# Attention and mixture-of-experts on one core: the first loads cut by the step that reads them, one buffer cleared by GpSimd, fewer unread products

## The chip, the core and the metric

The kernel runs on one core of a Trainium2 chip. The core has TensorE (PE, and PEld for its weight loads), VectorE (DVE), ScalarE (ACT), GpSimd (POOL) and SyncE (SP, which here issues most DMAs), and 16 DMA engines. The metric is the device time of one execution in microseconds (us): the median of several runs.

## The reference

Windowed attention feeds a routed mixture of experts. The attention part, cut to what matters:

```python
scores = scale * np.matmul(q, k.transpose(0, 1, 3, 2))      # q, k, v: 8 x 8 heads x 576 x 64
rel = pos[:, None] - pos[None, :]
mask_plain = (rel >= 0) & (rel < 32)                        # heads 0 to 3
mask_dil = (rel >= 0) & (rel < 128) & (rel % 4 == 0)        # heads 4 to 7
scores = np.where(masks[None, :, :, :], scores, -1000000000.0)
attn = np.exp(scores - np.max(scores, axis=-1, keepdims=True))
attn = attn / (np.sum(attn, axis=-1, keepdims=True) + 1e-09)
x = np.matmul(attn, v)                                      # then 4608 tokens of 512 numbers
# each token goes to one of 4 groups and one of its 4 experts, by the largest logit;
# out = g_w * e_w * (relu(x @ w1[g, e]) @ w2[g, e])
```

## The kernel before

The attention part is a loop over 36 steps, s = 0 to 35, written out by hand. Three steps share a load group g = s // 3, and a step takes the part jl = s % 3 of it. `qb[g % 3]` holds the group's queries, `kb[g % 2]` its keys, `vt[g % 3]` its values. The third buffers of q and v lie in the two weight buffers `wa`, so the trace calls `vt[2]` "wa". Step 0 reads its keys from a small buffer of its own, `k0t`, which also lies in "wa".

Pass s of the loop issues, on TensorE: a product that writes the masks into the score buffer (L254), the scores of step s (L273), the product of step s - 2's probabilities with the values (`av`, L315), the transposes of step s - 1's probabilities (L303), and those of step s - 3's result (L393). VectorE takes the maximum of the scores and subtracts it (L283, L285), ScalarE takes the exponential (L296) and copies the transposed probabilities out (L304). So the scores of step 3 stand ahead of `av` of step 1, in the same pass.

`keep_busy(n)` issues n products of the masks (L239) into a buffer that nothing reads, after the mask product of steps 0 and 1.

`av` reads the values twice: as loaded (`vt`) and shifted by half a block (`vs`). GpSimd makes `vs` with `shift_v`: the even half (partitions 64 to 127) takes the same part j of the group, the odd half takes part j - 1, or the last part of the group before. For group 0 it is called as `shift_v(0, 0, 1)` and `shift_v(0, 1, 3)`, so one GpSimd instruction makes the even half of parts 1 and 2 together (64x2x1040, which the trace calls 64x2080).

`carry_k(g)` fills the first 256 columns of `kb`. For every third group, GpSimd clears them (L119, 128x2x256, 128x512 in the trace); otherwise ScalarE copies them from the other buffer (L121). The clearing for group 3 writes `kb[1]`, whose first columns step 3 of group 1 reads.

TensorE, VectorE, ScalarE and SyncE follow the order of the program text here or a hand order; on GpSimd a scheduler of the language places the instructions, and each engine works through its own list in that order. SP issues the loads in the order in which they are written. `masks` comes in two DMAs: parts 0 and 1 by ACT, parts 2 to 5 by POOL; step 2 is the first that reads part 2.

```python
load_q(0, 1, 3)
load_k(0)
load_v(0, (0, 1, 3))
nc.gpsimd.dma_start(masks[:, 2:], cm[:, 2:])
load_k(1)
load_q(1)
load_q(2)
load_v(1)
```

After the steps come the routing of the last tokens, the choice of experts, and 18 pieces of expert work, with matmuls all the way.

Of the kernel before, what the change touches and what calls it, by code (L numbers as in the profile page):

```python
# [17 lines left out]
P = 128  # L18
# [38 lines left out]
def moe_attention_kernel(ctx, tc, q, k, k0, v, cmask, wgate, wpack, out):  # L57
    nc = tc.nc
# [34 lines left out]
    NQ, NK, NPT = 3, 2, 2  # L93
# [6 lines left out]
    vt = [qp.tile([P, 2, 3, 8, 65], F32, name=f"vt{i}") for i in range(2)]  # L100
    vt.append(wa32[1][:, 0:VW].rearrange("p (w j s c) -> p w j s c", w=2, j=3, s=8))
    vs = [qp.tile([P, 2, 3, 8, 65], F32, name=f"vs{i}") for i in range(2)]
    kb = [qp.tile([P, 2, KW], F32, name=f"kb{i}") for i in range(NK)]
# [6 lines left out]
    def load_q(g, j0=0, j1=3):  # L110
        nc.sync.dma_start(qb[three(g)][:, j0:j1], q[g, :, j0:j1])

    def load_k(g, halves=(0, 1)):
        for w in halves:
            nc.sync.dma_start(kb[g % NK][w:P:2, w, 256:], k[g, w])

    def carry_k(g):
        if g % 3 == 0:
            nc.gpsimd.memset(kb[g % NK][:, :, 0:256], 0.0)  # L119
        else:  # L120
            nc.scalar.copy(kb[g % NK][:, :, 0:256], kb[(g - 1) % NK][:, :, 3 * 256 : 4 * 256])  # L121

    def load_v(g, cuts=(0, 3)):
        for j0, j1 in zip(cuts, cuts[1:]):
            for r in range(2):
                nc.sync.dma_start(vt[three(g)][r:P:2, r, j0:j1], v[g, 64 * r : 64 * r + 64, j0:j1])
# [20 lines left out]
    for i, t in enumerate(kb):  # L147
        nc.vector.memset(t[:, 0], 0.0)
        nc.scalar.activation(t[:, 1], id32[:, 0:1].broadcast_to([P, KW]), AF.Copy, scale=0.0)
        if i == 0:  # L150
            nc.vector.memset(vt[0][:, 0], 0.0)
            nc.gpsimd.memset(vt[0][:, 1], 0.0)
    flat = lambda t: t.rearrange("p w j s c -> p (w j s c)")
    nc.scalar.activation(flat(vt[1]), id32[:, 0:1].broadcast_to([P, VW]), AF.Copy, scale=0.0)
    for w in range(2):
        nc.sync.dma_start(k0t[w:P:2, w, 0 : 8 * 96], k0[w])
    load_q(0, 1, 3)
    load_k(0)
    load_v(0, (0, 1, 3))
    nc.gpsimd.dma_start(masks[:, 2:], cm[:, 2:])  # L160
    load_k(1)
    load_q(1)
    load_q(2)
    load_v(1)

# [68 lines left out]
    def keep_busy(n):  # L234

        t = psA.tile([P, 2, 512], F32, name="idle", tag="o")
        m = masks[:, 0:2].unsqueeze(1).broadcast_to([P, 2, 2, 128])
        for i in range(n):
            nc.tensor.matmul(t[:, i % 2].rearrange("p (u m c) -> p u m c", u=2, m=2), idb, m, start=True, stop=True)  # L239

    def slot():
        credit[0] = min(credit[0] + rate[0], 2 * rate[0])
        while routes and not gate and credit[0] > 0:
            took = run(routes)
            if took in (2, 3):
                gate.append(took)
            elif took not in (None, 1):
                credit[0] -= took

    def scores(n):  # L250
        g, jl, J = n // 3, n % 3, n % NJ
        s = psS.tile([P, 4, 2, 64], F32, name="s", tag="s")
        m = masks[:, MASK_OF.get(J, 1), :]
        nc.tensor.matmul(  # L254
            s.rearrange("p (t u) w k -> p t (u w) k", t=2),
            idb,
            m.rearrange("p (t k) -> p t k", t=2).unsqueeze(2).broadcast_to([P, 2, 4, 64]),
            start=True,
            stop=False,
        )  # L260
        if n < 2:
            keep_busy((3, 10)[n])
        qv = qb[three(g)][:, jl]
        if n == 0:
            kv, ev0 = k0t[:, :, 0 : 8 * 96].rearrange("p w (s b k) -> p w b s k", s=8, k=32), 2
        else:
            kv, ev0 = kb[g % NK].rearrange("p w (b s k) -> p w b s k", s=8, k=32), 4
        for c in range(4):
            for bb in range(2):
                for a in range(2):  # L270
                    sl, j = bb * 4 + c, bb * 2 + a
                    first, step = jl + a, ev0 - a
                    nc.tensor.matmul(  # L273
                        s[32 * j : 32 * j + 32, c].rearrange("p w k -> p (w k)"),
                        qv[:, (sl * 2 + a) * 32 : (sl * 2 + a) * 32 + 32],
                        kv[:, :, first : first + step + 1 : step, sl],
                        start=False,
                        stop=(c == 3),
                    )
        s = s.rearrange("p c w k -> p (c w) k")  # L280
        d = ap.tile([P, 4, 64, 2], F32, name="d", bufs=2)
        mx = ap.tile([P, 8], F32, name="mx")
        nc.vector.tensor_reduce(mx, s, axis=AX.X, op=ALU.max)  # L283
        slot()
        nc.vector.tensor_tensor(  # L285
            d.rearrange("p c k w -> p c w k"),
            s.rearrange("p (c w) k -> p c w k", w=2),
            mx.rearrange("p (c w) -> p c w", w=2).unsqueeze(3).broadcast_to([P, 4, 2, 64]),
            ALU.subtract,
        )  # L290
        slot()
        dd[n] = d

    def softexp(n):
        p = dd.pop(n)
        nc.scalar.activation(p, p, AF.Exp, scale=SCALE)  # L296
        st[n] = p

    def transpose_p(n):
        p = st.pop(n)  # L300
        t = psT[0].tile([P, 4, P], F32, name="t", tag="t")
        for c in range(4):
            nc.tensor.transpose(t[:, c, :], p[:, c].rearrange("p k w -> p (k w)"), id32)  # L303
        nc.scalar.copy(pt[n % NPT], t)  # L304

    def av(n):
        g, jl = n // 3, n % 3
        o = psA.tile([P, 2, 512], F32, name="o", tag="o")
        for c in range(4):
            for bb in range(2):  # L310
                for a in range(2):
                    j = bb * 2 + a
                    t = vt[three(g)] if a else vs[g % 2]
                    at = 130 * (c % 2)
                    nc.tensor.matmul(  # L315
                        o[32 * j : 32 * j + 32, c // 2, at : at + 130],
                        pt[n % NPT][:, c, 32 * j : 32 * j + 32],
                        t[:, :, jl, bb * 4 + c, :],
                        start=True,
                        stop=True,  # L320
                    )
        oo[n] = o
# [589 lines left out]
    def expert(r):  # L912
        ev[r] = nc.sync.value_load(ordi[0:1, r : r + 1], min_val=0, max_val=NE - 1)
# [36 lines left out]
    for s in range(NT + 3):  # L950
        ripe = bool(gate)
        if s < NT:
            scores(s)
        if s % 3 == 2 and s // 3 + 2 < NT // 3:
            load_k(s // 3 + 2, (0,))
        if s % 3 == 0 and 2 <= s // 3 + 1 < NT // 3:
            load_k(s // 3 + 1, (1,))
        if s % 3 == 1 and 1 <= s // 3 + 1 < NT // 3:
            carry_k(s // 3 + 1)
        if s % 3 == 0 and NQ <= s // 3 + 2 < NG:  # L960
            load_q(s // 3 + 2) if s // 3 + 2 < NG - 1 else None
        if s // 3 + 2 == NG - 1:
            load_q(NG - 1, s % 3, s % 3 + 1)
        if 0 <= s - 2 < NT:
            av(s - 2)
            if ripe:
                gate.clear()
        if start:
            n = start[0]
            routes.append(route(n, turned_logits(n)))  # L970
            rate[0] = RATE[n]
        if 0 <= s - 1 < NT:
            transpose_p(s - 1)
        if s < NT:
            softexp(s)
        if s == 0:
            nc.vector.memset(flat(vt[2]), 0.0)
        if 0 <= s - 3 < NT:
            transpose_x(s - 3)
        if s % 3 == 1 and 2 <= s // 3 + 2 < NG - 1:  # L980
            load_v(s // 3 + 2)
        if s // 3 + 1 == NG - 1 and s % 3 < 2:
            load_v(NG - 1, ((0, 2), (2, 3))[s % 3])
        if 0 <= s - 2 < NT:
            normalise(s - 2)
        if start:
            n = start.pop()
        if gate == [3]:
            gate.clear()
        slot()  # L990
        if s % 3 == 0 and s // 3 + 1 < NT // 3:
            shift_v(s // 3 + 1, 0, 2)
        if s % 3 == 1 and s // 3 + 1 < NT // 3:
            shift_v(s // 3 + 1, 2, 3)
        for r in picked:
            if r not in ev:
                expert(r)
        if s == min(WSTEPS):
            wq.append(prefetch())
        if s == NT - 1:  # L1000
            eb.append(early(0, new_x(fe, EARLY[0]), fe, EARLY[0]))
        run(eb, EARLY_STEPS.get(s, 0))
        run(wq, WSTEPS.get(s, 1))
        if s >= 3 and (s - 3) % NJ == NJ - 1:
            bp = (s - 3) // NJ
            if bp < NBP - 1:
                start.append(bp)
        run(eq)
# [242 lines left out]
```

## Time and profile before

| | |
|---|---|
| median of 3 runs | 556.91 us (556.44 to 557.72) |
| profiled execution | 565.16 us, its span 563.4 us |
| TensorE busy | 537.1 us, 95% of the span |
| VectorE, ScalarE, GpSimd busy | 66%, 56%, 43% |
| attention steps | first product at 4.17 us, the masks of step 35 at 136.27 us |
| memory | 106.16 MB read, 19.29 MB written |

The span is what the profiler saw of the program; the execution's own time holds 1.8 us more. A busy share counts an instruction from its start to its modelled end. In a row of the timeline, "[1.00 <-DMA qb<-q]" says that the engine stood idle for 1.00 us before the row and that a landing of q into qb ended it. The queue of an engine that issues DMAs is written with a q: SPq, POOLq, ACTq.

### The profile page before, as it was taken

Reading aid. Unit: us, or ns where it says so; the run is one execution under the profiler, and the core shown is the slowest. Engines: PE = TensorE matmul, PEld = TensorE weight load, DVE = VectorE, ACT = ScalarE, POOL = GpSimd, SP = SyncE. Lnnn points to the kernel's source line nnn. Section 1 sums busy time; section 2 is a strip of 40 time slices with the busy share of each in tenths; the row PEclk is TensorE's granted clock in tenths of the full one; section 3 lists DMA queues with packets and bytes.
Section 4 is the critical chain, followed back from the end, with each engine's and each line's share of the span. In section 5 each row is a group of like instructions: output and inputs, shape, how many; then the busy total and the mean of one; then the engine's idle time right before and its main releaser. Section 6 shows DMA issues by size and latency. Waiting matters only on the chain. (4 is left out here: it accounts for less than half of the span.)

```text
span 563.4 us, 16475 instructions
## 1 busy us (share of the span) xinstructions
PE 537.1 (95%) x6577; PEld 384.8 (68%) x6577; DVE 369.9 (66%) x842; ACT 316.3 (56%) x563; POOL 241.1 (43%) x219
## 2 busy tenths in 40 slices
PE   6899999998898999999999999999999999999995
PEld 4777878786765765657666667575656756787883
DVE  8776786877787226574859597755647477658640
ACT  6555556567663335564646565564646567647741
POOL 6796566758958232603041513224160531221212
PEclk9999999999999999999999999999999999999999
DMA  8988988798592716978787786979697699898841
GB/s 284 407 288 278 320 268 279 233 317 290 162 305 55 259 41 127 335 180 258 185 286 165 271 211 226 255 225 293 175 315 199 217 295 276 293 333 229 257 113 30
DMA packets 79265, 134.31 MB, mean 238 GB/s; under 512 B 42988, under 2 KB 52630, under 8 KB 79186
## 3 DMA queue, kind: packets, MB, share of 16 engines
q1 hardware_dynamic: 72258, 113.65, 66.5%
q0 software_dynamic: 6784, 19.51, 10.4%
q8 instruction: 53, 0.87, 0.6%
q14 instruction: 26, 0.21, 0.1%
q10 hardware_dynamic: 144, 0.07, 0.0%
HBM read 106.16 MB, written 19.29 MB: 223 GB/s over the span
## 5 line engine op out<-in xcount | busy, mean ns | idle before, releaser
L818 POOL DMA_INDIRECT out<-yr,sent x31 | 38.4, 1238 | 220.0 <-ACT yr L817 202.0
L762 DVE SCALAR_TENSOR_TENSOR hl<-a,hh 128x256 f16<-128x256 f32 (+13 forms) x144 | 60.7, 424 | 97.6 <-ACT hh L761 77.4
L754 PE MATMUL a<-xs,wb1h 128*128 128x256 f16 (+7 forms) x576 | 97.9, 275 | 2.6 <-DVE hl L762 2.5
L754 PE MATMUL a<-xs,wa 128*128 128x304 f16 (+7 forms) x864 | 97.5, 272 | 1.5 <-issue 0.8
L761 ACT ACTIVATE hh<-a 128x256 f16<-128x256 f32 (+13 forms) x144 | 55.4, 388 | 72.1 <-PE a L754 55.3
L754 PEld LDWEIGHTS <-wa 128*128 128x128 f16 x864 | 79.0, 98 | 19.0 <-issue 2.5
L847 PEld LDWEIGHTS <-hh 128*128 128x128 f16 x480 | 46.9, 98 | 54.7 <-issue 1.2
L663 DVE SCALAR_TENSOR_TENSOR wa<-w,wa 128x1024 f16<-128x1024 f32 x57 | 69.1, 1230 | 18.5 <-ACT wa L667 14.6
L754 PE MATMUL a<-xs,wb1l 128*128 128x256 f16 (+7 forms) x288 | 78.3, 275 | 0.0
L847 PE MATMUL y<-wa,hh 128*128 128x512 f16 x240 | 73.9, 379 | 0.5 <-issue 0.5
L667 ACT ACTIVATE wa<-w 128x1024 f16<-128x1024 f32 x64 | 66.9, 1055 | 11.3 <-DMA w<-wpack 8.8
L754 PEld LDWEIGHTS <-wb1h 128*128 128x128 f16 x576 | 55.0, 98 | 15.6 <-issue 3.4
L817 ACT ACTIVATE yr<-y,cs 128x512 f32<-128x512 f32 (+3 forms) x31 | 21.3, 687 | 56.1 <-issue 26.4
L693 POOL DMA_INDIRECT xr<-xd,sent x41 | 42.1, 1026 | 19.2 <-issue 11.0
L847 PE MATMUL y<-wb2h,hh 128*128 128x512 f16 x120 | 45.6, 380 | 0.0
L847 PE MATMUL y<-wb2h,hl 128*128 128x512 f16 x120 | 45.5, 379 | 0.0
L847 PE MATMUL y<-wb2l,hh 128*128 128x512 f16 x120 | 45.5, 379 | 0.0
L847 PE MATMUL y<-wa,hl 128*128 128x512 f16 x120 | 45.5, 379 | 0.0
L663 DVE SCALAR_TENSOR_TENSOR wb2l<-w,wb2h 128x1024 f16<-128x1024 f32 x29 | 36.3, 1281 | 13.7 <-ACT wb2h L667 13.7
L304 ACT COPY pt<-t 128x512 f32<-128x512 f32 x36 | 21.0, 584 | 37.8 <-PE t L303 37.7
L315 PE MATMUL o<-vs,pt 128*32 128x130 f32 x576 | 39.9, 273 | 2.3 <-DVE own L498 0.9
L283 DVE TENSOR_REDUCE mx<-s 128x8 f32<-128x512 f32 x36 | 24.7, 687 | 24.5 <-PE s L273 24.4
(207 smaller groups left out, 1088.2 us busy)
## 6 DMA issues: line engine op xcount, KB each, us to landing
w<-wpack SPq DMA_DIRECT2D x128, 512.0 KB
kb<-k SPq DMA_DIRECT2D x24, 384.0 KB
vt<-v SPq DMA_DIRECT2D x14, 390.0 KB
qb<-q SPq DMA_DIRECT2D x7, 768.0 KB
xd<-x SPq DMA_DIRECT2D x24, 192.0 KB
wa<-v SPq DMA_DIRECT2D x6, 390.0 KB
wa<-q SPq DMA_DIRECT2D x3, 768.0 KB
xd<-x SPq DMA_DIRECT2D x32, 48.0 KB
```

The lines of the kernel that those rows point to most:

```text
L283: nc.vector.tensor_reduce(mx, s, axis=AX.X, op=ALU.max)
L304: nc.scalar.copy(pt[n % NPT], t)
L315: nc.tensor.matmul(o[32 * j : 32 * j + 32, c // 2, at : at + 130], pt[n % NPT][:, c, 32 * j : 32 * j + 32], t[:, :, jl, bb * 4 + c, :], st ...
L663: nc.vector.scalar_tensor_tensor(l, w32, SW, h, ALU.mult, ALU.subtract)
L667: nc.scalar.mul(parts(i)[0], w32s[i], SW)
L693: nc.gpsimd.indirect_dma_start(out=xr[0:n], out_offset=None, in_=xd[0:known, :], in_offset=bass.IndirectOffsetOnAxis(ap=ent[0:n, t : t + 1 ...
L754: nc.tensor.matmul(a[:, 0:cap], ww[:, c * FF + f * P : c * FF + f * P + P], xx[:, c, 0:cap], start=(i == 0), stop=(i == len(mm) - 1),)
L761: nc.scalar.activation(hh[:, f, 0:cap], a[:, 0:cap], AF.Relu)
L762: nc.vector.scalar_tensor_tensor(hl[:, f, 0:cap], a[:, 0:cap], 0.0, hh[:, f, 0:cap], ALU.max, ALU.subtract)
L817: nc.scalar.activation(yr[0:n, :], yp[0:n, :], AF.Copy, scale=cs[0:n, t : t + 1])
L818: ins = nc.gpsimd.indirect_dma_start(out=out, out_offset=bass.IndirectOffsetOnAxis(ap=ent[0:n, t : t + 1], axis=0), in_=yr[0:n, :], in_off ...
L847: nc.tensor.matmul(yp, h[:, f, t * P : t * P + n], ww[:, f * DM : f * DM + DM], start=(i == 0), stop=(i == len(mm) - 1),)
```

## The change

Three things change. The loads of group 0 and group 1 are cut by the part that a step reads, and go out in the order of the steps (`load_k_part` is new); one column block of `kb[0]` that no step reads is not loaded any more. The clearing of `vt[2]` moves from VectorE, behind step 0, to GpSimd, ahead of the DMA of masks 2 to 5. `keep_busy` of step 1 issues 1 product instead of 10; that of step 0 keeps its 3.

```diff
+    def load_k_part(g, j0, j1, h0=0, h1=2):
+
+        part = lambda a: a.rearrange("p (h c) -> p h c", h=2)[:, h0:h1, 256 * j0 : 256 * j1]
+        for w in range(2):
+            nc.sync.dma_start(part(kb[g % NK][w:P:2, w, 256:]), part(k[g, w]))
+
...
             nc.gpsimd.memset(vt[0][:, 1], 0.0)
+            nc.gpsimd.memset(vt[2].rearrange("p w j s c -> p (w j s c)"), 0.0)
...
-    load_q(0, 1, 3)
-    load_k(0)
-    load_v(0, (0, 1, 3))
+    load_q(0, 1, 2)
+    load_k_part(0, 1, 2)
+    load_k_part(0, 0, 1, 0, 1)
+    load_v(0, (0, 1))
+    load_q(0, 2, 3)
+    load_k_part(0, 2, 3)
+    load_v(0, (1, 2))
     nc.gpsimd.dma_start(masks[:, 2:], cm[:, 2:])
-    load_k(1)
-    load_q(1)
+    load_k_part(1, 0, 1)
+    load_q(1, 0, 1)
+    load_v(0, (2, 3))
+    load_k_part(1, 1, 3)
+    load_q(1, 1, 3)
     load_q(2)
     load_v(1)
...
-            keep_busy((3, 10)[n])
+            keep_busy((3, 1)[n])
...
-        if s == 0:
-            nc.vector.memset(flat(vt[2]), 0.0)
```

The order of the instructions shows three places. On SP, at the start of the program before the change, each row is one DMA, or two where it ends in x2:

```order
L111 DMA qb0_108<-q 128x512
L156 DMA wa0_91<-k0 64x768 x2
L111 DMA qb0_108<-q 128x1024
L115 DMA kb0_114<-k 64x1536 x2
L126 DMA vt0_110<-v 64x520 x2
L126 DMA vt0_110<-v 64x1040 x2
L115 DMA kb1_115<-k 64x1536 x2
L111 DMA qb1_109<-q 128x1536
L111 DMA wa0_91<-q 128x1536
L126 DMA vt1_111<-v 64x1560 x2
```

And on SP with the change, down to the same values of group 1:

```order
L111 DMA qb0_108<-q 128x512
L163 DMA wa0_91<-k0 64x768 x2
L111 DMA qb0_108<-q 128x512
L121 DMA kb0_114<-k 64x2x256 x2
L121 DMA kb0_114<-k 64x256 x2
L132 DMA vt0_110<-v 64x520 x2
L111 DMA qb0_108<-q 128x512
L121 DMA kb0_114<-k 64x2x256 x2
L132 DMA vt0_110<-v 64x520 x2
L121 DMA kb1_115<-k 64x2x256 x2
L111 DMA qb1_109<-q 128x512
L132 DMA vt0_110<-v 64x520 x2
```

The queries of group 1 that step 3 reads were part of the 13th DMA on SP and are now the 18th; the DMAs ahead of them are smaller.

On GpSimd, the opening of the program with the change; `wa1` is where `vt[2]` lies:

```order
L152 MEMSET wa0_91 128x768
L158 MEMSET vt0_110 128x1560
L159 MEMSET wa1_92 128x3120
L171 DMA masks_89<-cmask 128x512
L183 AFFINE_SELECT upper_161<-ones_159 128x128
```

Before, the row of `wa1` was not there, and the DMA of the masks followed the clearing of `vt0` at once.

On GpSimd a little later, the shifts of group 0's values and what follows them, before the change:

```order
L136 MEMSET vs0_112 64x2x520
L131 TENSOR_SCALAR vs0_112<-vt0_110 64x2x520
L134 TENSOR_SCALAR vs0_112<-vt0_110 64x2x520
L131 TENSOR_SCALAR vs0_112<-vt0_110 64x2x1040
L134 TENSOR_SCALAR vs0_112<-vt0_110 64x2x520
L138 TENSOR_SCALAR vs1_113<-vt0_110 64x2x520
L119 MEMSET kb1_115 128x2x256
```

And with the change (L137 is the even half, L140 the odd one, L125 the clearing by `carry_k`):

```order
L142 MEMSET vs0_112 64x2x520
L137 TENSOR_SCALAR vs0_112<-vt0_110 64x2x520
L140 TENSOR_SCALAR vs0_112<-vt0_110 64x2x520 x2
L125 MEMSET kb1_115 128x2x256
L137 TENSOR_SCALAR vs0_112<-vt0_110 64x2x1040
L144 TENSOR_SCALAR vs1_113<-vt0_110 64x2x520
```

The clearing of `kb1`'s first columns for group 3 stood behind all shifts of group 0; it now stands ahead of the one that makes the even half of parts 1 and 2. On VectorE, ScalarE and TensorE nothing else moves, but that a copy of 128x64 (`low`) now follows the first maximum on VectorE instead of standing ahead of it.

## Rows read from the trace of the kernel before

**Rows 1.** The page's busy times: engine, us, share of the span, instructions.

```profile
PE 537.1 (95%) x6577; PEld 384.8 (68%) x6577; DVE 369.9 (66%) x842; ACT 316.3 (56%) x563; POOL 241.1 (43%) x219
```

**Rows 2.** Timeline of PE, 0 to 20 us: start, us, operation, idle before.

```profile
4.17 0.59 PE L254 MATMUL s<-masks,idb 128*128 128x512 bf16 x1 [4.17 <-DMA masks<-cmask]
...
8.01 0.61 PE L254 MATMUL s<-masks,idb 128*128 128x512 bf16 x1
8.41 2.58 PE L239 MATMUL idle<-masks,idb 128*128 128x512 bf16 x10
10.92 1.08 PE L273 MATMUL s<-kb,qb 128*32 128x128 f32 x32
11.94 0.66 PE L303 MATMUL t<-id,d 128*128 128x128 f32 x4
12.43 0.38 PE L254 MATMUL s<-masks,idb 128*128 128x512 bf16 x1
12.74 1.08 PE L273 MATMUL s<-kb,qb 128*32 128x128 f32 x32
13.63 0.27 PE L315 MATMUL o<-vs,pt 128*32 128x130 f32 x1
...
15.28 0.66 PE L303 MATMUL t<-id,d 128*128 128x128 f32 x4 [0.58 <-ACT d L296]
...
17.16 1.08 PE L273 MATMUL s<-kb,qb 128*32 128x128 f32 x32 [1.00 <-DMA qb<-q]
18.03 0.27 PE L315 MATMUL o<-vs,pt 128*32 128x130 f32 x1
```

**Rows 3.** All waits of PE between 20 and 45 us: total, times, longest.

```profile
PE s L273 <- issue: 0.4, 1, 0.4
```

**Rows 4.** Busy time by engine, 10 to 15 us; last: granted clock, DMA share, GB/s.

```profile
10.00:15.00 5.00, 4.70 (x106) 3.26 (x104) 4.37 (x5) 2.24 (x4) 3.67 (x4) 1.00 1.04 424
```

**Rows 5.** Timelines of ACT and DVE, 0 to 20 us.

```profile
0.78 0.40 ACTq L143 DMA_DIRECT2D masks<-cmask  x1
...
10.05 0.63 ACT L296 ACTIVATE d<-d 128x512 f32<-128x512 f32 x1 [1.48 <-DVE d L285]
...
10.62 2.66 DVE L977 MEMSET wa<- 128x3120 f32 x1 [0.60 <-issue]
```

**Rows 6.** Timeline of POOL, 0 to 24 us.

```profile
2.33 1.39 POOL L152 MEMSET vt<- 128x1560 f32 x1
3.67 0.73 POOL L160 DMA_DIRECT2D masks<-cmask  x1
7.31 0.29 POOL L169 TENSOR_SCALAR_AFFINE_SELECT upper<-ones 128x128 bf16<-128x128 bf16 x1 [2.90 <-DVE own L181]
...
13.81 1.93 POOL L131 TENSOR_SCALAR vs<-vt 64x2080 f32<-64x2080 f32 x1
15.82 1.05 POOL L134 TENSOR_SCALAR vs<-vt 64x1040 f32<-64x1040 f32 x1
...
18.39 0.53 POOL L119 MEMSET kb<- 128x512 f32 x1 [0.50 <-PE s L273]
20.98 1.93 POOL L131 TENSOR_SCALAR vs<-vt 64x2080 f32<-64x2080 f32 x1 [2.06 <-DMA vt<-v]
```

**Rows 7.** Timelines of SP in short stretches from 5.2 to 10.5 us.

```profile
5.24 0.47 SPq L126 DMA_DIRECT2D vt<-v  x1
...
8.43 0.54 SPq L115 DMA_DIRECT2D kb<-k  x1
9.78 0.33 SPq L111 DMA_DIRECT2D qb<-q  x1
```

**Rows 8.** POOL's DMA queue, 6.85 to 9.25 us: packets, MB, share; none earlier or later.

```profile
q0 software_dynamic: 48, 0.13, 14.6%
```

**Rows 9.** A hand-over from POOL to PE late in the steps, timeline from 100 us.

```profile
100.93 1.05 POOL L134 TENSOR_SCALAR vs<-vt 64x1040 f32<-64x1040 f32 x1
...
102.27 0.14 PEld L315 LDWEIGHTS o<-vs,pt 128*32 128x32 f32 x2 [0.60 <-POOL vs L134]
```

## The prediction, made before the changed kernel ran

> **What bounds the kernel now.** First the busy times: TensorE works 537.1 of 563.4 us [rows 1], so there are only 26 us to win on it, or work to take from it. The change touches the start alone, so I read TensorE's timeline of the first 20 us [rows 2]. Three things there are not needed work. Ten unread products run from 8.41 for 2.58 us ahead of the scores of step 1. The transposes of step 1 wait 0.58 us for an exponential, which is late because VectorE clears a buffer for 2.66 us from 10.62 [rows 5]. And the scores of step 3 wait 1.00 us for the queries of group 1. Behind `av` of step 1, at 18.03, there is almost nothing: in the 25 us from 20 on TensorE waits 0.4 us in all [rows 3]. So whatever time `av` of step 1 starts at, later steps follow it one for one. The whole effect is read from that one start: 18.03 before.
>
> **The unread products.** Nine of ten go: 9 x 0.258 = 2.3 us of TensorE's work [rows 2]. What hides behind them is the landing of step 1's keys, which the trace does not show. With the change they are the 7th and 8th DMA of SP. The 7th went out at 5.24 and the 12th at 8.43, so one costs SP 0.64 us [rows 7], and the 8th is out by 5.9. The shortest way from an issue to a use in these rows is that of the first masks, 0.78 to 4.17, 3.39 us [rows 5, 2]; the longest that of the queries of group 1, 9.78 to 17.16, 7.38 us, with full queues [rows 7, 2]. I take the short one, for little is queued by then: scores of step 1 at 9.3 at the latest, done at 10.35. Next on TensorE are the transposes of step 0, and they need the exponential of step 0, done at 10.05 + 0.63 = 10.68 [rows 5], which the change leaves alone. So the transposes start at 10.7, not 11.94: 1.2 us won here, not 2.3.
>
> **The clearing on VectorE.** It goes from VectorE, so the maximum of step 1 follows its scores and the 0.58 us vanish.
>
> **The clearing on GpSimd.** The nearest row is half as large: 1.39 us for 128x1560 [rows 6], so 2.8 us. GpSimd has 2.90 us idle ahead of 7.31 [rows 6], which cover it; without them it would push the shifts. But the DMA of masks 2 to 5 stands behind it and goes out at 3.67 + 2.8 = 6.45. Before, its 48 packets all ran between 6.85 and 9.25 [rows 8], that is 3.2 to 5.6 us after the issue; now 9.6 to 12.0. Step 2 is the first reader, and TensorE is ready for its mask product at 10.7 + 0.49 = 11.2 [rows 2]. So this costs 0 to 0.8 us.
>
> **TensorE's way to step 3.** From the mask product of step 2: 1.20 to `av` of step 0, 1.07 to the transposes of step 1 (15.28 less 13.63, without the 0.58), 0.49 to the mask product of step 3, 0.31 to its scores: 3.07 us [rows 2]. So TensorE is ready for the scores of step 3 between 14.3 and 15.1.
>
> **The loads of step 3.** The queries of group 1 are the 18th DMA. From the 7th at 5.24, at 0.64 each, that is 12.3; an issue of q takes only 0.33 [rows 7], and the 7th no longer stands behind VectorE's third clearing, so I take 11.8. Plus 3.39 is 15.2; plus 7.38 would be 19.2. I take the short one: the 7th to the 18th DMA carry 64 to 256 KB each, 1672 KB together by their shapes, in 12 x 0.64 us, about 220 GB/s, while the engines moved 424 GB/s at a full share of 1.04 [rows 4], so no queue builds up. Scores of step 3 then start at 15.2 instead of 17.16: 2.0 us won up to here.
>
> **What GpSimd does with it.** The order shows what decides: the clearing of `kb1`'s first columns now stands ahead of the shift of parts 1 and 2 of group 0. That clearing overwrites what the scores of step 3 read. Before, it was released by those scores, at 18.39, 1.23 us after their start at 17.16 [rows 6, 2], and nothing needed it soon: the shift of parts 1 and 2 had run at 13.81. Now that shift is queued behind it, and `av` of step 1 waits for the shift. From the start of step 3's scores: 1.23, then the clearing 0.53, a gap of 0.08 (13.81 + 1.93 to 15.82), the shift 1.93 [rows 6], and the hand-over to TensorE 0.29 (100.93 + 1.05 to 102.27) [rows 9]: 4.06 us, where TensorE alone needed 0.87. So `av` of step 1 starts at 15.2 + 4.06 = 19.3, against 18.03: 1.2 us later. All that was won is paid back, and more. Break-even needs the scores of step 3 at 13.97, which TensorE's own way (14.3) does not reach; from 15.08 on the loss is over 1.1 us.
>
> **Behind it.** The shift of group 1's first values began at 20.98 on their landing [rows 6] and ends at 22.9. GpSimd is free for it at about 20.1 (19.0 plus one shift of 1.05). Its reader is two steps behind `av` of step 1, at 19.3 + 2 x 2.76 = 24.8, so a landing 1.9 us later would still be hidden. The loads of step 3's group that are not needed at once go out later than before, but their readers stand behind the same `av`.
>
> **Sum.** On the profiled execution: 565.16 + 1.2 = 566.4 us. That one is 8 us over the median of the plain runs, 556.91; I carry the difference over unchanged: 558.1 us. About 0.2%, 1.1 us, is what a measurement of this kernel can tell from no change, so the likeliest value lies on that border.
>
> **Rivals.**
> - *Issuing is cheap* (0.27). If the cut costs SP no time, the 18th DMA is out when the 13th was, at 9.78, lands by 13.2, and TensorE's own way decides: scores of step 3 at 14.3 to 15.0, `av` of step 1 0.3 to 1.0 late, 557.5 us: same. For it: a q issue of 0.33; against it: six issues in a row at 0.64. The Trainium skill, "DMA: Bandwidth & Descriptors", section "Issuing engines are not separate DMA queues", says that the issue time is usually small beside the DMA itself; by that rule this rival holds. The rows differ for pieces this small: 128 KB at 424 GB/s is 0.31 us, half of its issue.
> - *Loads arrive late* (0.10). If the queue is half as full as before, 5.4 us from issue to use: scores of step 3 at 17.2, `av` of step 1 at 21.3, 560.1 us: slower. Against it stands the thinner supply.
> - *The clock* (0.08). The same mask product took 0.61 at 8.01 and 0.38 at 12.43 [rows 2]: TensorE worked at the lower of its two levels (1.2 GHz) first and, after unbroken work from 4.17 on, at the upper one (2.4 GHz), where the granted clock is 1.00 [rows 4]. With one product instead of ten, TensorE has gaps from 10 us on, the longest some 3 us ahead of `av` of step 1. If it rises later or falls back, a step (mask product 0.38 to 0.61, the rest alike by 1.6) loses about 1.7 us; with one step at the lower level 559.8 us: slower. The Trainium skill, "TensorE: Matmul & The Clock Gate", section "What's actually happening", says that the default state is throttled and that activity releases it; that speaks for this rival. Against it: the ground up to 8.7 is the same as before.
> - *GpSimd does not hold it* (0.07). The wait of the clearing was put down to the scores of step 3, but a wait for several is put down to the last. If it need not wait for them, `av` of step 1 follows its program order and TensorE is 17.16 less 14.3 = 2.9 us ahead: 554.0 us: faster. It decides if the clearing runs ahead of those scores.
> - The forecast (0.48): scores of step 3 at 14.9 to 15.7, 557.8 to 558.6 us; 0.30 of it lies over the border, 0.18 under.
>
> **Numbers.** Faster: 0.07. Same: 0.27 + 0.18 = 0.45. Slower: 0.30 + 0.10 + 0.08 = 0.48. The range runs from 556.7, just under the cheap-issue case's 557.2, to 560.2, which takes in the clock and the late loads; the faster rival and worse tails stay out.
>
> **What would show it.** In the changed profile: mask product of step 2 at 11.2 to 12.2; transposes of step 0 at 10.7; scores of step 3 at about 15.2; then GpSimd's clearing of `kb` at 16.4, its 64x2080 shift ending at 19.0, and `av` of step 1 waiting some 3 us on it, at 19.3; from there on every step 1.2 us later than before. SP's issues of the cut loads should stand 0.6 us apart. Wrong would be: `av` of step 1 before 17, no wait on GpSimd there, a mask product of 0.6 us behind 12 us, or a later wait that takes the delay back.

## The result, and the profile after

The changed kernel takes 564.72 us (median of 4 runs, 564.09 to 571.62), the kernel before 557.32 us beside it (4 runs): a ratio of 1.0128, 95% interval 1.0078 to 1.0177. It is slower by 7 us; I had forecast 1.2. The profiled execution of the changed kernel took 564.09 us, its span is 562.3 us. That of before, with 563.4, was a long one of its kernel: a second profile of the same kernel, the first experiment below, has a span of 556.6 us, and its rows of the first 20 us lie within 1 us of the first profile's. So 562.3 less 556.6, 5.7 us, is what two profiles show of the loss. Nearly all of it lies ahead of step 28. The masks of that step in the second profile of before, and then with the change:

```profile
107.02 0.38 PE L254 MATMUL s<-masks,idb 128*128 128x512 bf16 x1
112.27 0.38 PE L268 MATMUL s<-masks,idb 128*128 128x512 bf16 x1
```

That is 5.25 us, and 4.4 against the first profile of before (107.85). What comes behind this row can't be told apart: there the two profiles of the one kernel before differ by 6.0 us.

TensorE's timeline with the change, to be read beside [rows 2] (start, us, operation, idle before):

```profile
8.86 1.08 PE L287 MATMUL s<-kb,qb 128*32 128x128 f32 x32 [0.24 <-DVE tab L229]
10.61 0.66 PE L317 MATMUL t<-id,d 128*128 128x128 f32 x4 [0.66 <-ACT d L310]
11.10 0.38 PE L268 MATMUL s<-masks,idb 128*128 128x512 bf16 x1
12.30 1.08 PE L287 MATMUL s<-kb,qb 128*32 128x128 f32 x32 [0.82 <-DMA kb<-k]
...
14.66 0.66 PE L317 MATMUL t<-id,d 128*128 128x128 f32 x4
15.15 0.38 PE L268 MATMUL s<-masks,idb 128*128 128x512 bf16 x1
15.94 1.08 PE L287 MATMUL s<-kb,qb 128*32 128x128 f32 x32 [0.41 <-DMA qb<-q]
19.76 0.42 PE L329 MATMUL o<-vs,pt 128*32 128x130 f32 x1 [2.74 <-POOL vs L137]
...
23.51 0.63 PE L268 MATMUL s<-masks,idb 128*128 128x512 bf16 x1
24.08 1.70 PE L287 MATMUL s<-kb,qb 128*32 128x128 f32 x32
```

The scores of steps 1, 2 and 3 start earlier than before; `av` of step 1 waits 2.74 us on GpSimd and starts at 19.76, 1.73 us late. So far it is the forecast. Then the delay grows: the scores of step 4 start at 24.08. Here is that row of before:

```profile
20.29 1.08 PE L273 MATMUL s<-kb,qb 128*32 128x128 f32 x32
```

That is 3.8 us late, where the forecast had every later step 1.2 us late. Step 4 itself runs partly at the lower clock (0.51, in the windows below), and the masks of step 5 are 4.4 us late (27.52 against 23.12), those of step 28 still 4.4 to 5.3. Behind the 2.74 us TensorE's waits up to 60 us are 0.8 and 0.2 us, no more than before (1.0 and 0.4 from 20 us on). GpSimd's timeline after, beside [rows 6]:

```profile
3.66 2.69 POOL L159 MEMSET wa<- 128x3120 f32 x1
6.31 0.74 POOL L171 DMA_DIRECT2D masks<-cmask  x1
...
17.17 0.53 POOL L125 MEMSET kb<- 128x512 f32 x1 [2.75 <-PE s L287]
17.79 1.92 POOL L137 TENSOR_SCALAR vs<-vt 64x2080 f32<-64x2080 f32 x1
...
25.55 1.92 POOL L137 TENSOR_SCALAR vs<-vt 64x2080 f32<-64x2080 f32 x1 [4.71 <-DMA vt<-v]
```

The last row is the shift of group 1's first values. It starts on their landing, at 25.55 instead of 20.98 [rows 6]: 4.57 us later. In this execution TensorE did not wait for it: it was late itself by then, and `av` of step 3, the first product that reads these values, starts at 28.73 without a wait. Why the values are late is in the transfers. Windows of the changed kernel; the last three numbers are the granted clock, the share of the DMA engines and GB/s:

```profile
5.00:10.00 5.00, 4.66 (x68) 2.49 (x66) 4.52 (x46) 3.65 (x3) 4.74 (x10) 1.00 0.84 251
10.00:15.00 5.00, 3.44 (x72) 2.64 (x73) 2.84 (x5) 2.19 (x4) 3.52 (x4) 1.00 0.82 239
15.00:18.50 3.50, 1.61 (x36) 0.98 (x34) 2.19 (x4) 1.11 (x2) 1.24 (x2) 1.00 0.96 293
18.50:25.50 7.00, 5.74 (x72) 4.62 (x75) 1.15 (x4) 2.33 (x5) 2.26 (x2) 0.51 1.00 376
```

Between 10 and 15 us the DMA engines move 239 GB/s at a share of 0.82; before it was 424 at 1.04 [rows 4]. All packets of the first 20 us, in the kernel before:

```profile
DMA packets 1907, 6.45 MB, mean 323 GB/s; under 512 B 305, under 2 KB 553, under 8 KB 1906
```

and with the change:

```profile
DMA packets 2900, 4.65 MB, mean 233 GB/s; under 512 B 398, under 2 KB 1422, under 8 KB 2899
```

More packets, 1.8 MB less (0.13 MB of it is the block that is no longer loaded). At the 424 GB/s of the full engines [rows 4] the other 1.67 MB are 3.9 us of transfer, most of the 4.57 us by which group 1's values are late. What SyncE waited for in those 20 us, in the second profile of the kernel before (total, times, longest):

```profile
SPq L115 <- DMA qb<-q: 1.8, 2, 1.4
SPq L111 <- DMA kb<-k: 1.6, 2, 1.0
SPq L115 <- DMA wa<-q: 1.3, 1, 1.3
```

and with the change, where these two rows are all:

```profile
SPq L163 <- DVE wa L151: 0.5, 1, 0.5
SPq L1253 <- PEq L1253: 0.5, 1, 0.5
```

Before, SyncE had issued ahead and waited for landings. With the change it waits for no landing in 20 us: it issues one DMA after the other, 0.63 us each (10.71 to 11.98 for two, below), and the engines run short. Group 1's values go out at 17.11 instead of 11.96 (second profile of before, its row below):

```profile
10.71 1.22 SPq L121 DMA_DIRECT2D kb<-k  x2
11.98 0.58 SPq L111 DMA_DIRECT2D qb<-q  x1
12.61 1.12 SPq L132 DMA_DIRECT2D vt<-v  x2
...
17.11 1.13 SPq L132 DMA_DIRECT2D vt<-v  x2
```

### The profile page after: what moved, and what is told of

Read it like the earlier page. It is cut to its first block, busy times and chain, and to the rows that moved or that the text cites. A ratio compares the mean times of both kernels' runs of the same rounds, so it can differ in the third digit from the quotient of the medians.

```text
span 562.3 us, 16473 instructions
## 1 busy us (share of the span) xinstructions
PE 535.3 (95%) x6568; PEld 385.7 (69%) x6568; DVE 366.6 (65%) x841; ACT 316.5 (56%) x563; POOL 239.6 (43%) x220
## 5 line engine op out<-in xcount | busy, mean ns | idle before, releaser
L832 POOL DMA_INDIRECT out<-yr,sent x31 | 34.1, 1099 | 221.1 <-ACT yr L831 203.6
L768 PEld LDWEIGHTS <-wb1h 128*128 128x128 f16 x576 | 55.1, 98 | 15.2 <-issue 2.9
L707 POOL DMA_INDIRECT xr<-xd,sent x41 | 42.4, 1034 | 19.3 <-issue 9.5
```

The source lines that it names most:

```text
L707: nc.gpsimd.indirect_dma_start(out=xr[0:n], out_offset=None, in_=xd[0:known, :], in_offset=bass.IndirectOffsetOnAxis(ap=ent[0:n, t : t + 1 ...
L768: nc.tensor.matmul(a[:, 0:cap], ww[:, c * FF + f * P : c * FF + f * P + P], xx[:, c, 0:cap], start=(i == 0), stop=(i == len(mm) - 1),)
L832: ins = nc.gpsimd.indirect_dma_start(out=out, out_offset=bass.IndirectOffsetOnAxis(ap=ent[0:n, t : t + 1], axis=0), in_=yr[0:n, :], in_off ...
```

## The experiments

Ratios are to the kernel before on the same chip, with their 95% intervals. The theory at the outset: GpSimd's hold as predicted, made worse by TensorE's clock, which was 0.51 from 18.5 to 25.5 us. Rivals: the cut loads deliver less; or the single product and the new place of the clearing.

**The kernel before, once more** (nothing edited).

> The kernel before, unchanged, for a second trace of it: the profiled execution of before took 565.16 us where its plain runs took 556.4 to 559.9. Both theories: an execution of 556 to 558 us, scores of step 3 near 17.2, av of step 1 near 18.0, values of group 1 landing near 21, no fall of TensorE's clock; the early part as in the first trace, the expert part some 8 us shorter.

558.35 us, just over what was expected, span 556.6; scores of step 3 at 17.35, the shift of group 1's values at 21.17, and 6 us less from step 28 to the end. Its windows, for comparison with the runs below, and SyncE's issue of group 1's values:

```profile
5.00:10.00 5.00, 4.56 (x41) 2.29 (x40) 4.59 (x46) 3.57 (x2) 2.69 (x8) 1.00 0.93 301
10.00:15.00 5.00, 4.39 (x98) 3.16 (x100) 4.30 (x5) 2.25 (x4) 2.87 (x4) 1.00 1.03 419
```

```profile
11.96 1.12 SPq L126 DMA_DIRECT2D vt<-v  x2
```

**The cut loads alone, and all but the cut loads.** The first has the new loads and nothing else of the change; its diff is against the changed kernel. The second keeps the old loads and makes the other two edits, the same lines with their signs turned, against the kernel before.

```diff
-            nc.gpsimd.memset(vt[2].rearrange("p w j s c -> p (w j s c)"), 0.0)
-            keep_busy((3, 1)[n])
+            keep_busy((3, 10)[n])
+        if s == 0:
+            nc.vector.memset(flat(vt[2]), 0.0)
```

> Only the loads are cut; ten unread products and VectorE's clearing stay as before. Theory A (GpSimd's clearing ahead of the shift holds av of step 1, TensorE's gap lets the clock fall) and theory B (the cut loads bring group 1's values 4.6 us later) both say slow here, 562 to 566 us, since the cut alone moves the clearing. Rival C (the single product and the lost warm-up are what costs): 557 to 559 us, no fall of the clock.

> The other two edits without the cut: one product, GpSimd's clearing of vt[2]. Theories A and B: 556 to 558 us, since the clearing of kb1 stands behind the shifts again and the values of group 1 land near 21. Rival C: 560 us or more, with a clock that rises later or falls.

The cut loads alone: ratio 1.0078 (1.0039 to 1.0117). All but the cut loads: 1.0024 (0.9993 to 1.0054), no difference that can be told. (Its median, 560.25 us, is over the expected 556 to 558, but the kernel before took 559.46 on that chip.) TensorE's rows of the second:

```profile
11.01 1.08 PE L274 MATMUL s<-kb,qb 128*32 128x128 f32 x32 [2.21 <-DMA kb<-k]
...
17.06 1.08 PE L274 MATMUL s<-kb,qb 128*32 128x128 f32 x32 [1.46 <-DMA qb<-q]
```

Nine products less, and TensorE waits for the keys instead, 2.21 us, and then as before for the queries: the loads set these starts. The rival of the single product falls as the main cause; most of the loss is in the loads. That the other two edits add up to 0.5% is not excluded by these two intervals.

**GpSimd's hold taken out.** The changed kernel with the clearing for group 3 on VectorE.

```diff
-            nc.gpsimd.memset(kb[g % NK][:, :, 0:256], 0.0)
+            eng = nc.vector if g == 3 else nc.gpsimd
+            eng.memset(kb[g % NK][:, :, 0:256], 0.0)
```

> The changed kernel with the clearing of kb1 for group 3 on VectorE in step 7, so that GpSimd makes the shift of parts 1 and 2 as soon as its values are there. Theory A: av of step 1 near 17.9, no fall of the clock, 557 to 559 us. Theory B: av of step 1 earlier all the same, but the values of group 1 land near 25 and av of step 3 cannot start before 27.3 (24.3 before): 560 to 563 us.

Ratio 1.0115 (1.0072 to 1.0159): nothing is won, where my theory had the time of before and the rival 560 to 563 us (564.66 measured). TensorE:

```profile
15.78 1.08 PE L288 MATMUL s<-kb,qb 128*32 128x128 f32 x32
19.64 0.30 PE L330 MATMUL o<-vs,pt 128*32 128x130 f32 x1 [2.77 <-POOL vs L138]
...
27.32 0.30 PE L330 MATMUL o<-vs,pt 128*32 128x130 f32 x1 [1.10 <-POOL vs L138]
```

and what it waits for first on GpSimd:

```profile
17.66 1.92 POOL L138 TENSOR_SCALAR vs<-vt 64x2080 f32<-64x2080 f32 x1 [3.14 <-DMA vt<-v]
```

With the clearing gone, the same shift waits for the last part of group 0's values, which lands at 17.66; with it, it started at 17.79. The hold was there, and behind it stood a late load of the same price. The second wait, 1.10 us at `av` of step 3, is for the shift of group 1's late values. In this run the granted clock is 1.00 in every stretch to 35 us, and the time is the same: the clock isn't needed for the loss either. My theory falls as the whole account; the late bytes remain. But why are they late: the number of DMAs, or their small pieces (1 or 2 KB in each partition, 4 to 6 before)?

**Number of DMAs against size of pieces.** Both kernels are that of before with the loads of `k(0)`, `k(1)` and parts 1 and 2 of `q(0)` split into twice as many DMAs; the first splits by partitions and keeps the large pieces, the second by columns. The edit of the keys, shortened:

```diff
-    load_k(0)
+    # by partitions: rows_of = slice(64 * h + w, 64 * h + 64, 2)
+    nc.sync.dma_start(kb[g % NK][rows_of, w, 256:], k[g, w, 32 * h : 32 * h + 32])
+    # by columns: small = a.rearrange("p (x t c) -> p x t c", t=2, c=256)[:, :, t]
+    nc.sync.dma_start(small(kb[g % NK][w:P:2, w, 256:]), small(k[g, w]))
```

> The kernel before, with the loads of k of groups 0 and 1 and of parts 1 and 2 of q of group 0 each split in two by partitions: five more DMAs ahead of the queries of group 1, which become the 18th, with the same bytes, the same order and the same large pieces in each partition (4 to 6 KB). It tries SyncE's issuing alone. Theory (the small pieces make the supply thin, not the number of DMAs): in the stretch of 10 to 15 us the DMA engines move about 400 GB/s for each unit of their share, as before (419 at 1.03); the shift of group 1's values starts at 21 to 22 us, scores of step 3 within 1 us of 17.35, and the time is that of before within 1 us (557 to 560). Rival (SyncE's pace of 0.64 us for each DMA makes it thin): the share falls to about 0.8 at 10 to 15 us, values of group 1 land 3 to 4 us later, and the time is 3 to 6 us longer.

> As the kernel with more DMAs, in number, bytes and order, but the same loads are split by columns: each DMA has pieces of 1 KB in each partition instead of 4 to 6 KB. Beside that run it tries the size of the pieces alone. Theory (small pieces): the engines are as busy but move about 290 GB/s for each unit of their share in 10 to 15 us (after: 239 at 0.82), the values of group 1 land 1.5 to 2.5 us later than in the run with large pieces, and the time is 2 to 3 us longer than its time. Rival (issuing): no difference between the two.

By partitions: 1.0076 (1.0046 to 1.0106). By columns: 1.0035 (1.0010 to 1.0060). The theory of small pieces missed both: it had no loss from the first, and the second slower than the first. The rival, issuing, had 3 to 6 us for the first (4.3 measured), but by a share of about 0.8, and the share was 1.04. If anything the large pieces are the slower ones (the intervals overlap), so small pieces are not the cause by themselves, and five DMAs more cost something in either form. Their windows, by partitions first:

```profile
10.00:15.00 5.00, 3.65 (x45) 1.92 (x43) 3.36 (x3) 1.33 (x3) 1.62 (x3) 1.00 1.04 281
```

```profile
10.00:15.00 5.00, 4.18 (x102) 3.13 (x101) 4.36 (x5) 2.19 (x4) 3.22 (x4) 1.00 0.90 291
```

The first is no clean test of issuing: its engines are full (1.04) and still move a third less than 419, something that a split by partitions brings of its own. In the second the engines stand idle a tenth of the time, and a unit of their share moves 291 / 0.90 = 323 GB/s, against 419 / 1.03 = 407. That is no measure of the pieces: the kernel before itself has 301 / 0.93 = 324 between 5 and 10 us, and the run of tiny DMAs below, with large pieces, 204 / 0.71 = 287.

**One cut alone, and the values first.** The kernel before with the queries of group 1 as part 0 and parts 1 and 2; and the changed kernel with group 1's values ahead of group 2's queries.

```diff
-    load_q(1)
+    load_q(1, 0, 1)
+    load_q(1, 1, 3)
...
+    load_v(1)
     load_q(2)
-    load_v(1)
```

> The kernel before, with one load cut: the queries of group 1 go as part 0, which step 3 reads, and then parts 1 and 2. One DMA more, pieces of 2 and 4 KB instead of 6. Theory (the loads set the pace of the steps, a step's start gains nothing that the later loads don't give back): scores of step 3 up to 1.2 us earlier, the time as before (within 1 us). Rival (the start of step 3 decides, and later steps follow one for one, as the prediction had it): 1 us faster.

> The changed kernel, with the values of group 1 issued ahead of the queries of group 2 instead of behind them. Theory (the bytes that the cut loads did not move by 20 us are missing for every load behind them): the values of group 1 land about 1.9 us earlier (786 KB at about 400 GB/s), GpSimd shifts them at 23.5 instead of 25.55, and the time stays within 1.5 us of the changed kernel (563 to 565). Rival (the late values of group 1 alone carry the loss): 2 us or more is won, 562.5 or less.

The single cut: 0.9964 (0.9933 to 0.9995), 2 us; scores of step 3 start at 16.07 without a wait. The theory had no gain there, so it missed by a little. In the profile the gain is 1.0 us at the masks of step 4 (19.19 against 20.18) and gone at those of step 28 (108.00 against 107.02). Values first: 1.0112 (1.0076 to 1.0149), as the changed kernel, though its shift comes 1.55 us earlier than there:

```profile
24.00 1.92 POOL L137 TENSOR_SCALAR vs<-vt 64x2080 f32<-64x2080 f32 x1 [2.49 <-DMA vt<-v]
```

So group 1's late values alone don't carry the loss.

**Issuing alone.** The kernel before, all real loads as they were, with eleven tiny DMAs strewn between them that nothing reads: of 64 rows, and of 16. Shortened:

```diff
+    crumbs = qp.tile([P, 11, 8], F32, name="crumbs")
+    # 2, 3, 3 and 3 of these behind q(0), k(0), v(0) and k(1); 16 rows in the second kernel
+    nc.sync.dma_start(crumbs[0:64, n], k[7, 0, 0:64, 8 * n : 8 * n + 8])
```

> The kernel before, with eleven tiny DMAs more on SyncE's queue (64 rows of 32 bytes each, into a buffer that nothing reads), spread over the places where the change adds DMAs ahead of the values of group 1. The real loads keep their pieces and order. It tries the number of DMAs that SyncE issues alone. Theory (SyncE's issuing, 0.63 us for each DMA, makes the supply thin): the values of group 1 are issued about 5 us later than at 11.96 (11 x 0.63 = 6.9 less what SyncE waited before), GpSimd shifts them at 25 instead of 21.2, and the time is 5 to 6 us longer than before, near a ratio of 1.01. Rival (the small pieces of the cut loads make it thin): SyncE is late too, but the engines catch up; the time is within 1.5 us of before.

> As the run with eleven tiny DMAs, but each of 16 rows instead of 64. If an issue takes SyncE as long for 16 rows as for 64, both runs cost the same; if it is shorter, the values of group 1 are issued earlier and the loss is smaller in proportion. By the theory of SyncE's issuing the loss follows the time at which the values of group 1 are issued; by the rival neither run loses.

With 64 rows: 1.0154 (1.0128 to 1.0179). With 16 rows: 1.0135 (1.0098 to 1.0172). Eleven DMAs that carry next to nothing cost as much as the change (the intervals overlap), and more than the 5 to 6 us expected. Window, SyncE, TensorE and GpSimd of the first:

```profile
10.00:15.00 5.00, 4.85 (x107) 3.29 (x104) 4.37 (x5) 2.26 (x4) 3.41 (x4) 1.00 0.71 204
```

```profile
17.33 1.46 SPq L126 DMA_DIRECT2D vt<-v  x2
```

```profile
21.29 1.08 PE L283 MATMUL s<-kb,qb 128*32 128x128 f32 x16 [5.16 <-DMA qb<-q]
```

```profile
25.31 1.93 POOL L131 TENSOR_SCALAR vs<-vt 64x2080 f32<-64x2080 f32 x1 [1.39 <-DMA vt<-v]
```

204 GB/s at a share of 0.71; group 1's values issued at 17.33 and shifted at 25.31: the picture of the changed kernel (17.11 and 25.55), without its pieces, order, clearing or products. TensorE's wait is another one, though: 5.16 us for the queries of step 3, which go out at 16.17 here and in the changed kernel at 11.98. With 16 rows an issue is a little shorter (0.50 against 0.62 us), group 1's values go out at 16.35 and are shifted at 25.04. The number of DMAs that SyncE issues is enough for a loss of this size; that the changed kernel loses by the same waits is not shown.

**The keys whole again.** The changed kernel with `load_k(0)` and `load_k(1)` in place of the `load_k_part` calls, six DMAs fewer on SyncE.

```diff
-    load_k_part(0, 1, 2)
-    load_k_part(0, 0, 1, 0, 1)
+    load_k(0)
...
-    load_k_part(0, 2, 3)
...
-    load_k_part(1, 0, 1)
+    load_k(1)
...
-    load_k_part(1, 1, 3)
```

> The changed kernel, with the keys of groups 0 and 1 loaded whole again (2 DMAs each instead of 6 and 4) and q and v cut as in the change: six DMAs fewer, and only 2 KB pieces left of the small ones. GpSimd's order is that of the changed kernel. Theory (SyncE's issuing): values of group 1 issued at 13.3 to 14 us instead of 17.11, shifted at 22 to 22.5 instead of 25.55, and the time 3 to 4 us shorter than that of the changed kernel, a ratio to before near 1.004. Rival (the order of the loads or GpSimd's order makes the loss): the time stays near that of the changed kernel, a ratio of 1.010 or more.

Ratio 1.0046 (1.0018 to 1.0074) instead of 1.0128: some 4.6 of 7 us come back. The run takes out six issues and the keys' small pieces together, so it doesn't tell these two apart. Group 1's values go out at 12.44, and the shift:

```profile
21.69 1.92 POOL L137 TENSOR_SCALAR vs<-vt 64x2080 f32<-64x2080 f32 x1 [0.59 <-DMA vt<-v]
```

Its engines move 354 GB/s at 1.01 from 10 to 15 us. What is left, 2.6 us, has the hold of the prediction in it: `av` of step 1 waits 2.8 us for that shift and starts at 20.02, and the clock is 0.66 from 20 to 25 us.

**Half the issues on another engine.** The changed kernel with the six DMAs of `v(0)` issued by ScalarE; `vt[1]` is cleared by GpSimd, `vt[2]` by VectorE behind step 0. In GpSimd's order the clearing of `kb1` then stands behind the shift. The edit, with one of the three calls of `load_v`:

```diff
-    load_v(0, (0, 1))
+    load_v(0, (0, 1), nc.scalar)
...
-            nc.gpsimd.memset(vt[2].rearrange("p w j s c -> p (w j s c)"), 0.0)
+            nc.gpsimd.memset(vt[1].rearrange("p w j s c -> p (w j s c)"), 0.0)
...
-    nc.scalar.activation(flat(vt[1]), id32[:, 0:1].broadcast_to([P, VW]), AF.Copy, scale=0.0)
...
+        if s == 0:
+            nc.vector.memset(flat(vt[2]), 0.0)
```

> The changed kernel with the same cut loads, but the six DMAs of group 0's values are issued by ScalarE, which has nothing to do between 5.9 and 9.9 us once its clearing of the second value buffer goes to GpSimd; the third is then cleared by VectorE behind step 0 as before the change. GpSimd's clearing of the keys' first columns stands behind the shift in this order, so the hold of the prediction is out too: its partner is the run with that clearing off GpSimd, ratio 1.0115. Theory (SyncE's issuing makes the supply thin): SyncE issues group 1's values about 3.8 us earlier than at 17.11, more moves than 239 GB/s between 10 and 15 us, GpSimd shifts group 1's values at 22 to 23 instead of 25.55, and the ratio to before falls to 0.998 to 1.006. Rival (the small pieces and the order make the loss, whoever issues them): 1.009 or more.

Ratio 1.0037 (1.0006 to 1.0067), where its partner without the hold had 1.0115: most of the loss is gone. But the steps behind it missed. SyncE issues group 1's values at 14.94, not 13.3, and the shift starts at 24.78, not 22 to 23:

```profile
10.00:15.00 5.00, 3.52 (x57) 2.53 (x61) 3.90 (x3) 2.28 (x4) 3.48 (x4) 0.68 0.92 293
```

```profile
SPq L121 <- DMA qb<-q: 1.5, 2, 1.3
...
SPq L121 <- DMA vt<-v: 1.1, 1, 1.1
```

```profile
5.25 6.66 ACTq L132 DMA_DIRECT2D vt<-v  x6
```

Six issues by ScalarE took 6.66 us, 1.11 each, and SyncE's loads of k waited for landings of q and v, data that they have nothing to do with. So with two engines issuing, it was landings that held the next issue, and the engines still moved only 293 / 0.92 = 318 GB/s for a unit of share. That fewer issues by SyncE, with the same pieces, give the time back fits the theory; that they do so by the early landing of group 1's values is not shown.

**A version that beats both?** The single cut with the other two edits; the same, but with `keep_busy` left at ten products; and the single cut with `v(0)` issued by ScalarE (`vt[1]` cleared by GpSimd instead of ScalarE). The edit of the first:

```diff
+            nc.gpsimd.memset(vt[2].rearrange("p w j s c -> p (w j s c)"), 0.0)
...
-    load_q(1)
+    load_q(1, 0, 1)
+    load_q(1, 1, 3)
...
-            keep_busy((3, 10)[n])
+            keep_busy((3, 1)[n])
...
-        if s == 0:
-            nc.vector.memset(flat(vt[2]), 0.0)
```

> The kernel before with the queries of group 1 cut in two (as in the run that did this alone, ratio 0.9964), the third value buffer cleared by GpSimd and one unread product ahead of step 1: the two parts of the change that cost nothing, with one cut out of the many. The loads' theory: they set the pace of the early steps, so the shorter way of TensorE brings nothing over the single cut: a ratio of 0.995 to 0.999. Rival (TensorE's start decides): another 1 to 2 us are won, a ratio of 0.993 or less.

> As the run with the queries of group 1 cut and the rest of the change (ratio 1.0055), but with ten unread products again. Its trace showed the granted clock at 0.54 between 10 and 15 us behind a wait of 3.13 us for the keys. Theory (the ten products cover that wait, and the lower clock cost 2 us): no granted clock under 1 before 40 us, scores of step 3 near 16.1 instead of 18.48, a ratio of 0.996 to 1.000. Rival (the clock and the products don't matter to the end): 1.003 or more.

> The kernel before with the queries of group 1 cut in two and the four DMAs of group 0's values issued by ScalarE (the second value buffer cleared by GpSimd instead of ScalarE): a version that may beat both kernels. Theory (the loads set the pace, and with large pieces the engines were already full from 10 us on): the share of 5 to 10 us rises from 0.93, scores of step 1 and 3 start up to 1 us earlier, a ratio of 0.993 to 0.999. Rival (TensorE's start decides nothing later): 1.000 within its interval.

One product: 1.0055 (1.0034 to 1.0075); both sides had a gain and missed. Ten: 0.9977 (0.9945 to 1.0009), as the theory had it. The third: 1.0000 (0.9976 to 1.0025), where the theory had a gain and missed. Windows of the first and the second:

```profile
10.00:15.00 5.00, 3.85 (x49) 2.84 (x53) 1.38 (x2) 2.00 (x4) 3.31 (x4) 0.54 1.02 413
```

```profile
10.00:15.00 5.00, 5.00 (x108) 3.39 (x106) 2.08 (x3) 2.39 (x4) 3.08 (x4) 1.00 1.04 402
```

With one product TensorE waits 3.13 us for the keys of step 1 and then works at the lower clock; with ten it works through, and the clock stays at 1.00. Scores of step 3 start at 18.48 against 15.93. But most of these 2.5 us is made up later. The masks of step 28, one product first:

```profile
107.14 0.38 PE L256 MATMUL s<-masks,idb 128*128 128x512 bf16 x1
106.55 0.38 PE L256 MATMUL s<-masks,idb 128*128 128x512 bf16 x1
```

The spans, 558.2 and 555.4 us, differ by 2.8 us, of which 0.6 lies ahead of this row, and with one product it comes no later than before (107.02 and 107.85). So the ratios differ, and that the early wait and the clock make the difference is not shown. No version is clearly faster than the kernel before but the single cut, whose interval ends at 0.9995.

## Why the prediction was wrong

**Unread products.** Right: the transposes of step 0 at 10.61, predicted 10.7. That the nine products cost nothing but time is in doubt where keys come late: the pair above differs by 0.8%, though its profiles don't show the cause.

**Clearing off VectorE, clearing on GpSimd.** Right: the 0.58 us vanished; GpSimd's clearing takes 2.69 us (2.8), the masks' DMA goes out at 6.31 (6.45), the mask product of step 2 runs at 11.10, so it cost nothing. The wait of 0.82 us for the keys of step 2 at 12.30 was not in the sum; TensorE was ready for step 3 at 15.5, not 14.3 to 15.1.

**Loads of step 3.** The 18th DMA went out at 11.98 (11.8) and the scores followed at 15.94 (15.2): 3.96 us of way instead of 3.39. The rule of the Trainium skill that I weighed ("DMA: Bandwidth & Descriptors", section "Issuing engines are not separate DMA queues"), that the issue time is usually small beside the DMA, does not hold for pieces this small: issues by SyncE stand 0.63 us apart, the run of tiny DMAs shows issuing alone at 1.0154, and the cheap-issue rival is out.

**GpSimd's hold.** Right in place, order and size: clearing at 17.17, shift at 17.79, `av` of step 1 at 19.76 (19.3). But it was not the bound alone: without it the shift waits for its own values until 17.66. I had asked when group 1's queries land, and not when the last part of group 0's values does, which goes out behind them at 12.61.

**The step that failed** is the sentence "about 220 GB/s, while the engines moved 424 GB/s at a full share of 1.04 [rows 4], so no queue builds up". The number was good (239 measured) and its meaning was missed: the engines had been full, so every GB/s under 424 is missing for the loads behind. What the runs showed in its place: SyncE's issues, 0.63 us each, set the supply. Eleven tiny issues more cost 1.0154 by themselves, and six issues moved from SyncE to ScalarE bring 1.0115 down to 1.0037. Two further sentences failed. "A landing 1.9 us later would still be hidden": it came 4.57 us later. In the changed kernel's profile TensorE was too late itself to wait for it; without the hold it waited 1.10 us. (The 2.76 us for a step in that sum stand in no row: the scores of steps 4 and 5 of the kernel before start at 20.29 and 23.43, 3.14 us apart, which makes the slack 2.7 us and not 1.9.) "Later steps follow it one for one": 1.73 us at `av` of step 1 became 3.8 at the scores of step 4, by the clock (below), which the sum had at nothing. The bytes of the first 20 us go with the ratio, but loosely: 6.37 to 6.45 MB where the ratio is at most 1.0024, 6.17 MB at 1.0046 (keys whole), 5.74 at 1.0035 (split by columns), 4.57 to 4.84 MB at 1.0112 to 1.0154. Off this line stand the cut loads alone (4.34 MB, 1.0078), half the issues on ScalarE (5.03 MB, 1.0037), the split by partitions (4.88 MB, 1.0076) and the single cut with one product (6.20 MB, 1.0055, with the lower clock), so these bytes are no measure by themselves.

**Rivals.** The clock did fall in the profiled run, to 0.51, during the wait of 2.74 us: from `av` of step 1 to the scores of step 4 it took 24.08 less 19.76, 4.32 us, against 20.29 less 18.03 [rows 2], 2.26: 2.1 us, near the 1.7 that this rival had. With the 1.73 of `av` of step 1 that is the whole delay of 3.8 us at step 4. In the run without the hold the clock stayed at 1.00, other waits came (1.1 us more on GpSimd and 0.9 us for keys by 60 us), and the total was the same. I gave late loads 0.10, and put their price on step 3 alone, not on what comes behind.

**What stays open:** how the loss divides between the hold with the clock and the late loads. In the changed kernel's own profile the hold and the clock fill the delay up to step 5. Without the hold and with the clock at 1.00 the masks of step 28 start later still, at 114.14 against 112.27, by waits for loads: it seems that each of the two covers the other. The profiles, single executions, also go with the ratio only roughly: step 28 starts at 114.42 with the cut loads alone (1.0078), at 110.02 with the values first (1.0112). Open too is what small pieces cost. From 10 to 15 us the changed kernel is 180 GB/s under the kernel before (419 less 239); at 407 GB/s for a unit of share, the 0.21 of share account for 85 of it. The rest is a lower rate for a unit of share (291), but the tiny DMAs with large pieces have that as well (287), so it doesn't speak for the pieces. And what a split by partitions does to the engines is open.

## What to carry to other kernels

When transfers are cut so that the first piece comes sooner, count the DMAs and multiply by the issue time (0.63 us here). Where that exceeds what the same bytes take at the engines' full rate, as here, the loads behind the cut go out later. Try the cut of the one load that a step waits for (the queries of group 1: 0.9964, the only ratio whose interval lies under 1) before cutting all of them. And when one hold is priced, ask for every input of the held instruction when it would come without it.

## What was not expected of the hardware

- **DMA engines can be full and slow.** Loads split by partitions (32 at a time): a share of 1.04 and 281 GB/s, where whole loads moved 419 at 1.03. The Trainium skill ("DMA: Bandwidth & Descriptors", section "Rules for kernel authors") advises against two transfers to partition halves because they share the same engines; here the split kernel did not come out even, but lost: 1.0076, with five DMAs more in it.
- **A second issuing engine didn't double the pace.** ScalarE needed 1.11 us for each of six issues beside SyncE, whose own then waited for landings of other loads.
- **Waits of one length left different clocks.** Behind 2.74 us idle the granted clock was 0.51 (the changed kernel), behind 2.77 us at the same place 1.00 (without the hold). Behind 3.13 us it was 0.54 (the single cut with one product), behind 2.21 us 1.00 (all but the cut loads).
